# Attention and two mixture-of-experts layers on one core: a new step order for the attention, zero fills issued by SyncE, early constants spread over three pairs, one condition at the end

## The chip, the cores and the metric

The kernel runs on one core of a Trainium2 chip. The metric is the device time of one execution in microseconds (us). A core has a matrix engine (PE in the profile, TensorE), VectorE (DVE), ScalarE (ACT), GpSimd (POOL) and SyncE (SP), which issues most DMA transfers. Each engine works through its own queue of instructions in a fixed order, and semaphores make one engine wait for another.

## What is computed

```python
# q, k, v: (4, 12, 448, 64); x of the first layer is the attention's output, (1792, 768)
q_n, k_n = rmsnorm(q, g_q), rmsnorm(k, g_k)
attn = softmax(q_n @ k_n.T / 8);  x = attn @ v
# layer 1: 8 experts, D=768, F=1024, each token goes to its best expert
logits = x @ w_gate; e = argmax(logits); gate = softmax(logits)[e]
x = gate * sigmoid(x @ w_output_gate)[e] * (relu(x @ w1[e]) @ w2[e])
# layer 2: the same without the output gate, with a bias per modality
logits = x @ w_gate2 + modality_bias[modality_id]; e = argmax(logits)
out = softmax(logits)[e] * (relu(x @ w1b[e]) @ w2b[e])
```

## The kernel before

The attention works on 24 pairs of heads (two heads side by side on the 128 partitions), six pairs to each of the 4 batches. `Attn.do(name, i)` issues one step of pair i. A step's name tells its work, and each belongs to one engine:

- `ld`, `ldv` (SP, L540/541): loads of q, k and v for two pairs. `nsq` (ACT, L560), `nss` (DVE, L565), `ny0` to `ny2` (ACT, L568 to L570), `nt1`, `nt2` (DVE, L574, L577), `nmul` (POOL, L583): the root mean square and the scaling.
- `tpe` (PE, L591), `thi` (ACT, L594/595), `tlo` (DVE, L598/599): transposes into Z, split into a high and a low half. `stk` (SP, L606/607): four DMAs copy Z into the stacked operand T.
- `mpe0` to `mpe3` (PE, L614/616): scores for the maximum, all in one PSUM buffer psm. `mred0` to `mred3` (DVE, L619/L620): the maximum of each row into m. `rpe` (PE, L626/627): m becomes a row; `rcp` (ACT, L629) copies that row into T.
- `spe` (PE, L637/638): the scores into PSUM pst. `exp` (ACT, L642). `lo` (POOL, some on DVE, L645): the exponentials' low half plo. `vhi`, `vlo` (L553, L555): v split. `pv` (PE, L655 to L657): the av matmuls, 24 to a block. `ev`, `es` (L660 to L667): division by the sum.
- `xpe`, `xcp`, `lpe`, `ladd`: transposes of the result and the router's logits. `store` (SP, L497/498).

`Attn.order` sorts all steps by a key, which is `i + OFF[step]`, or for pairs at both ends an entry of the table `PRO`. A third table, `EXT`, gives keys to what is placed among them: the routing of the third batch (`rb`, `ra`, `rk`, `rs`), the pick of the first expert (`pk`, `ex`) and its loads and splits (`ld`, `lw`, `wh`, `wl` and others). Twelve ticks a pair run `tick`: it issues set-up loads and the routing of the first two batches (small DVE steps, L89 to L156, a few per tick). `hook` issues one zero fill of the buffer yd (L76, 384 KB from a tile of zeros, on ACT's queue) for each of pairs 6 to 19. The program is issued in the order of the keys, and that is each engine's order. Constants (L42 to L54 and L810 to L818, on POOL) are made ahead of pair 0's steps.

Then units of tokens of one expert follow: `halves` multiplies with w1 (eight blocks), yields (the middle), and with w2 (six blocks), all by `mm3` (L356). A unit's last scatter (L365, POOL) is put off to the next unit, or issued by `flush`. In the middle of unit e3 stands a condition (L965) for rare further units, whose body isn't run here. The end:

```python
seq=S["B"][:4]+S["S"]
for j in range(4): M.unit(seq[j],nx=seq[j+1],fx=seq[j+2],...)
M.flush()
NS=nc.values_load(nsi[0:1,0:1],min_val=0,max_val=E)      # L983
NB=nc.values_load(nbi[0:1,0:1],min_val=0,max_val=G2)     # L984
# chains: with tc.If(NS>i): M.unit(S[i], now=True); chains(i+1)    L985 to L992
# chainb: with tc.If(NB>i): a further unit; chainb(i+1), from i=4   L993 to L999
```

With this input NS is 2 and NB is 4: units B0 to B3 (304 tokens each) run in straight code, S0 and S1 (128 each) in nested conditions, and the conditions for more are not taken.

Of the kernel before, what the change touches and what calls it, by code (L numbers as in the profile page):

```python
# [27 lines left out]
class Moe:  # L28
# [471 lines left out]
class Attn:  # L500
# [182 lines left out]
    OFF=dict(ld=-3.47005,nsq=-2.879,nss=-2.54025,ny0=-2.4295,ny1=-2.42643,ny2=-2.3877,nt1=-2.36309,nt2=-2.36284,nmul0=-2.04952,  # L683
        nmul1=-2.04952,tpe0=-1.91912,thi0=-1.82412,tlo0=-1.80912,tpe1=-1.73278,thi1=-1.55,tlo1=-1.52437,mpe0=-1.23853,mred0=-1.11883,mpe1=-0.89826,
        mred1=-0.61069,mpe2=-0.58025,mred2=-0.49799,stk=-0.40471,mpe3=-0.39269,mred3=-0.36259,rpe=-0.28877,rcp=-0.05802,spe0=0.03615,exp0=0.22883,
        spe1=0.2646,spe2=0.31037,spe3=0.4246,exp1=0.44482,lo0=0.48909,ldv=0.50817,exp2=0.56868,exp3=0.57203,vhi=0.58407,vlo=0.75941,
        lo1=0.82029,lo3=0.95048,lo4=0.95048,lo6=0.95048,lo2=1.02771,lo5=1.06696,pv0=1.36506,pv1=1.42944,pv2=1.67538,pv3=1.83832,
        ev0=2.0046,ev1=2.07284,ev2=2.12131,es=2.3119,xpe=2.51876,xcp=2.67122,lpe=3.17606,ladd=3.42453,store=5.55173)
# [340 lines left out]
```

## Time and profile before

| | |
|---|---|
| median of 3 runs (lowest to highest) | 931.42 us (931.07 to 934.42) |
| the profiled execution, its own time | 930.19 us |
| its span, first to last instruction | 928.5 us |
| mean granted clock of TensorE, share of full speed | 0.967 |

The profile is of one execution. Its page groups busy time by engine and by line; the trace behind it has each instruction with its start, its length, and how long its engine stood idle before it and for whom. The page's line numbers are those of the kernel before; in the changed kernel the attention's lines stand 7 later.

### The profile page before, as it was taken

What the parts mean: (1) busy time and instruction counts of PE and PEld (TensorE: products, weight loads), DVE (VectorE), ACT (ScalarE), POOL (GpSimd) and SP (SyncE); (2) the same over time, 40 slices, a digit from 0 to 9 for tenths busy, and PEclk for the clock granted to TensorE, in tenths of its full rate; (3) what the DMA queues carried; (4) which work ended last, traced back from release to release, by engine and by line L of the source; (5) the groups of instructions that cost most, each with busy time, mean ns of one, the idle gap of its engine ahead of it and who ended that gap; (6) DMA issues with size and microseconds to landing.
All of it is one profiled execution on the core that took longest, in us unless ns stands there. A gap on an engine that the chain in (4) does not pass through costs nothing. (4 is left out here: it accounts for less than half of the span.)

```text
span 928.5 us, 23302 instructions
## 1 busy us (share of the span) xinstructions
PE 852.6 (92%) x8881; PEld 664.3 (72%) x8881; DVE 679.9 (73%) x1405; ACT 527.6 (57%) x967; POOL 386.9 (42%) x404
## 2 busy tenths in 40 slices
PE   4699998998998899999999999989989999999990
PEld 1366665665655788777788999887757777777890
DVE  6688889888778774877788888788646675655670
ACT  4577776776766542655455566565436454544560
POOL 5686767867766422413144242524023331411200
PEclk9799999999999899999999999999989999999996
DMA  5577655764564646995868779976748778594640
GB/s 129 122 169 171 166 169 146 187 167 118 135 169 133 168 133 201 268 282 211 218 177 326 234 164 317 310 208 233 240 131 259 232 284 185 223 310 136 243 157 13
DMA packets 143946, 182.00 MB, mean 196 GB/s; under 512 B 73736, under 2 KB 111384, under 8 KB 143808
## 3 DMA queue, kind: packets, MB, share of 16 engines
q1 hardware_dynamic: 131904, 151.95, 55.3%
q0 software_dynamic: 6784, 22.32, 8.0%
q10 hardware_dynamic: 5120, 5.98, 1.9%
q8 instruction: 76, 1.25, 0.6%
q14 instruction: 62, 0.51, 0.2%
HBM read 130.12 MB, written 24.33 MB: 166 GB/s over the span
## 5 line engine op out<-in xcount | busy, mean ns | idle before, releaser
L356 PE MATMUL pl<-XT,w1h 128*128 128x304 bf16 (+7 forms) x1632 | 259.3, 268 | 1.1 <-issue 0.5
L356 PE MATMUL pl<-hl,w2h 128*128 128x304 bf16 (+7 forms) x816 | 213.5, 270 | 6.3 <-DVEq L965 3.7
L356 PE MATMUL pl<-hh,w2h 128*128 128x304 f16 (+7 forms) x816 | 213.2, 269 | 0.0
L356 PE MATMUL pl<-hh,w2l 128*128 128x304 f16 (+7 forms) x816 | 213.2, 269 | 0.0
L356 PE MATMUL pl<-XT,w1l 128*128 128x304 f16 (+7 forms) x816 | 211.6, 268 | 1.2 <-issue 1.0
L356 PEld LDWEIGHTS <-w2h 128*128 128x128 f16 x1632 | 150.9, 98 | 35.7 <-issue 5.4
L356 PEld LDWEIGHTS <-w1h 128*128 128x128 f16 x1632 | 150.0, 98 | 29.1 <-issue 3.3
L645 POOL TENSOR_TENSOR plo<-p 128x448 f16<-128x448 f32 x142 | 140.1, 1005 | 52.1 <-ACT p L642 47.6
L299 DVE TENSOR_TENSOR w1l<-r,w1h 128x1024 bf16<-128x1024 f32 x96 | 116.6, 1229 | 45.6 <-ACT w1h L298 43.2
L423 ACT COPY yt<-pl 128x304 f32<-128x304 f32 (+7 forms) x102 | 37.0, 363 | 154.3 <-PE pl L356 147.6
L345 POOL TENSOR_TENSOR XS<-xr,XS 128x768 bf16<-128x768 f32 (+5 forms) x27 | 47.9, 1794 | 149.9 <-ACT XS L344 149.9
L298 ACT CAST w1h<-r 128x1024 f16<-128x1024 f32 x96 | 99.6, 1054 | 0.1
L642 ACT ACTIVATE p<-pst,eb 128x896 f32<-128x896 f32 (+1 forms) x96 | 86.4, 911 | 17.7 <-PE pst L638 16.8
L359 ACT ACTIVATE hh<-pl 128x304 f16<-128x304 f32 (+7 forms) x136 | 50.5, 372 | 75.5 <-PE pl L356 66.5
L655 PE MATMUL av<-vv,p 128*128 128x65 f16 (+1 forms) x768 | 89.4, 199 | 2.0 <-ACT xrow L667 2.0
L356 PEld LDWEIGHTS <-w2l 128*128 128x128 bf16 x816 | 80.2, 98 | 13.2
L356 PEld LDWEIGHTS <-w1l 128*128 128x128 bf16 x816 | 79.8, 98 | 13.1 <-DVE w1l L299 0.4
L655 PEld LDWEIGHTS <-p 128*128 128x128 bf16 (+1 forms) x768 | 73.4, 102 | 20.8 <-issue 14.8
L657 PE MATMUL av<-vv,plo 128*128 128x65 f16 (+1 forms) x768 | 87.6, 195 | 0.6 <-DVE plo L645 0.6
L656 PE MATMUL av<-vv,p 128*128 128x64 f16 (+1 forms) x768 | 88.1, 197 | 0.0
L619 DVE TENSOR_REDUCE m<-psm 128x2 f16<-128x896 f32 x70 | 76.0, 1086 | 10.0 <-PE psm L614 7.9
L299 DVE TENSOR_TENSOR w2l<-raw,w2h 128x768 bf16<-128x768 f32 x64 | 71.8, 1121 | 9.5 <-ACT w2h L298 9.3
(297 smaller groups left out, 1661.8 us busy)
## 6 DMA issues: line engine op xcount, KB each, us to landing
r<-in_moe_w_dram SPq DMA_DIRECT2D x96, 512.0 KB
raw<-in_moe_w_dram SPq DMA_DIRECT2D x64, 384.0 KB
r2a<-in_moe_w_dram SPq DMA_DIRECT2D x32, 384.0 KB
r2b<-in_moe_w_dram SPq DMA_DIRECT2D x32, 384.0 KB
T<-Z SPq DMA_DIRECT2D x48, 224.0 KB
T<-Z SPq DMA_DIRECT2D x48, 112.0 KB
yd<-zero ACTq DMA_DIRECT2D x14, 384.0 KB
rv<-in_v_dram SPq DMA_DIRECT2D x24, 192.0 KB
```

The lines of the kernel that those rows point to most:

```text
L298: if part!=1: nc.scalar.copy(h,t)
L299: if part!=0: (eng or nc.vector).tensor_tensor(out=l,in0=t,in1=h,op=ALU.subtract)
L345: if part!=0: (eng or nc.vector).tensor_tensor(out=self.XS[:m,t,1].bitcast(BF16),in0=x,in1=h,op=ALU.subtract)
L356: self.nc.tensor.matmul(p,a,b,start=i==0,stop=i==tot-1); i+=1
L359: nc.scalar.activation(h,p,AF.Relu)
L423: nc.scalar.copy(self.yt[:,db,:N],p)
L619: if t<3: nc.vector.tensor_reduce(m[:,t:t+4:3],p[:,:,:S],axis=AX.X,op=ALU.max,negate=True)
L642: self.nc.scalar.activation(self.d["P",i][:,self.u(kt)],p[:,:nn,:S],AF.Exp,bias=self.eb,scale=0.125)
L645: eng.tensor_tensor(out=self.d["L",i][:,u],in0=P[:,u],in1=self.hi(P)[:,u],op=ALU.subtract)
L655: nc.tensor.matmul(o,hh,w[:,0:65],start=kt==0,stop=False)
L656: nc.tensor.matmul(o[:,0:64],hh,w[:,65:129],start=False,stop=False)
L657: nc.tensor.matmul(o,ll,w[:,0:65],start=False,stop=kt==3)
```

## The change

The tables `OFF`, `PRO` and `EXT` have new numbers, so the attention's steps stand in another order (`PRO` now covers pairs 0 to 3 and 17 to 23, before 0 to 4 and 18 to 23). The limits of the routing's ticks move with them. `blank` issues its fill on SP's queue and is called from `tick` at the fifth tick of a pair. `consts`, `set_caps` and `early` become generators, and one piece of them is issued per tick of pairs 1 to 3. At the end S0 and S1 run in straight code behind B3; VectorE works out `over`, the number of units beyond these, in B1; every engine loads it in S0, and one condition on it stands in the middle of S1, with all further units in its body.

```diff
@@ class Moe @@
     def consts(self):
...
+        yield
         self.e8m=iota("e8m",[128,E],[[1,E]],-8,0)
+        yield
...
     def blank(self,t,i,n):
...
-        self.nc.scalar.dma_start(out=t[i*(NT//n):(i+1)*(NT//n),:]...
+        self.nc.sync.dma_start(out=t[i*(NT//n):(i+1)*(NT//n),:]...
...
     def redo(self,u,nx):
...
-        u.e=e; self.fetch(nx,nx.slot); nx.e=None; self.bring(nx,0,3)
-        nx.e=None
+        u.e=e
+        if nx is not None: self.fetch(nx,nx.slot); nx.e=None; self.bring(nx,0,3); nx.e=None
@@ class Attn @@
-    OFF=dict(ld=-3.47005,nsq=-2.879,nss=-2.54025,ny0=-2.4295,...
+    OFF=dict(ld=-3.56465,nsq=-2.18384,nss=-1.88231,ny0=-1.59399,...
...
@@ body_full @@
-            M.consts()
+            yield from M.consts()
...
+            yield from M.set_caps(CAPS,((128,0),(N2,128)))
...
         def rk(p,i):
-            if S.get("w")=="rk" and i<19: S["w"]=S["r"].send(p)
+            if S.get("w")=="rk" and i<16: S["w"]=S["r"].send(p)
         def rr(i):
-            if S.get("w")=="r" and i<19: step()
+            if S.get("w")=="r" and i<16: step()
         def tick(i,s):
             if i==0 and s in (1,3,5): M.clear_rows(s//2)
+            if 1<=i<4: next(S["e"],None)
+            if s==4 and 6<=i<20: M.blank(yd,i-6,14)
...
-            if "r" in S and i<19 and (S.get("w") is None or S["w"]=="sc" and s in (2,10)): step()
+            if "r" in S and i<21 and (S.get("w") is None or S["w"]=="sc" and s in (2,6,10)): step()
         def hook(i,s):
-            if s==2 and 6<=i<20: M.blank(yd,i-6,14)
+            pass
...
-            early(); A.run(O=O,EXT=EXT,ext=ext)
+            S["e"]=early(); A.run(O=O,EXT=EXT,ext=ext)
...
-        seq=S["B"][:4]+S["S"]
-        for j in range(4): M.unit(seq[j],nx=seq[j+1],fx=seq[j+2],...
+        seq=S["B"][:4]+S["S"][:2]
+        (be,nbi),(se,nsi)=S["b2"],S["s2"]
+        over=cst.tile([128,1],I32,name="over")
+        def more():
+            a,b=[lp.tile([128,1],F32,name=n) for n in ("ova","ovb")]
+            nc.vector.tensor_scalar(a,nsi,-2.0,0.0,op0=ALU.add,op1=ALU.max); nc.vector.tensor_scalar(b,nbi,-4.0,0.0,op0=ALU.add,op1=ALU.max)
+            nc.vector.tensor_tensor(out=over,in0=a,in1=b,op=ALU.add)
+        def load(t,n): return nc.values_load(t[0:1,0:1],min_val=0,max_val=n)
+        def chain(n,i,m,unit):
+            if i>=m: return
+            with tc.If(n>i):
+                u=unit(i); cold(u); M.unit(u); M.flush()
+                chain(n,i+1,m,unit)
+        def others():
+            post,M.post,sl=M.post,None,M.slot
+            with tc.If(S["over"]>0):
+                chain(load(nsi,E),2,E,lambda i: Unit(L2,se,i,128))
+                chain(load(nbi,G2),4,G2,lambda i: Unit(L2,be,i,N2))
+                M.redo(seq[-1],None)
+            M.slot=sl; M.post=post
+        def known(): S["over"]=load(over,E+G2)
+        sides={0:{KF+i:[stepper("table3")] for i in range(6)},1:{2:[more]},4:{2:[known]}}
+        for j,u in enumerate(seq):
+            M.unit(u,nx=seq[j+1] if j<5 else None,fx=seq[j+2] if j<4 else None,side=sides.get(j),late=0,mid=others if j==5 else None)
         M.flush()
-        (be,nbi),(se,nsi)=S["b2"],S["s2"]
-        NS=nc.values_load(nsi[0:1,0:1],min_val=0,max_val=E)
...
-        chains(0)
...
-        chainb(4)
```

The tables' effect is seen in the order of instructions. First SP's queue near the start: T_148 is the stacked operand of pair 1, wgt the gate weights, raw_114 the q and k of pairs 4 and 5. Before:

```order
L606 DMA T_148<-Z_154 64x2x896
L607 DMA T_148<-Z_154 64x2x448
L606 DMA T_148<-Z_154 64x2x896
L607 DMA T_148<-Z_154 64x2x448
L822 DMA wgt<-in_moe_w_gate_dram 128x6x8
L823 DMA wgt<-in_moe_w_output_gate_dram 128x6x8
L540 DMA raw_114<-in_q_dram 64x4x256
L541 DMA raw_114<-in_q_dram 64x4x192
L540 DMA raw_114<-in_k_dram 64x4x256
L541 DMA raw_114<-in_k_dram 64x4x192
```

and after the change:

```order
L837 DMA wgt<-in_moe_w_gate_dram 128x6x8
L838 DMA wgt<-in_moe_w_output_gate_dram 128x6x8
L613 DMA T_148<-Z_154 64x2x896
L614 DMA T_148<-Z_154 64x2x448
L613 DMA T_148<-Z_154 64x2x896
L614 DMA T_148<-Z_154 64x2x448
L547 DMA raw_114<-in_q_dram 64x4x256
L548 DMA raw_114<-in_q_dram 64x4x192
L547 DMA raw_114<-in_k_dram 64x4x256
L548 DMA raw_114<-in_k_dram 64x4x192
```

The two loads of gate weights moved from behind pair 1's stacking to ahead of it. Next TensorE's queue where pair 10's row of maxima (m_155) is made; Z_153 is pair 10's operand, Z_154 pair 11's, p and plo the exponentials of an earlier pair. Before, its last maximum block (L616), a block of 24 av matmuls and the row:

```order
L616 LDWEIGHTS Z_153
L616 MATMUL psm<-Z_153 64x448
...
L655 LDWEIGHTS p_1935
L655 MATMUL av<-vv_139,p_1935 128x65
...
L657 LDWEIGHTS plo
L657 MATMUL av<-vv_139,plo 128x65
L626 LDWEIGHTS m_155
L626 MATMUL pmt<-id_157,m_155 1x128
```

After the change the row stands behind the second maximum block of pair 11 (the blocks ahead of that, back to pair 10's last maximum block, are scores, av, pair 11's first maximum block, a transpose and two blocks of av):

```order
L664 LDWEIGHTS plo
L664 MATMUL av<-vv_139,plo 128x65
L621 LDWEIGHTS Z_154
L621 MATMUL psm<-Z_154 128x448
L633 LDWEIGHTS m_155
L633 MATMUL pmt<-id_157,m_155 1x128
```

Last VectorE's queue at pair 10's fourth maximum (the reduction that fills one column of m_155, L620), while a batch is routed (rt names); m_156 is pair 11's. Before:

```order
L619 TENSOR_REDUCE m_155<-psm 128x2
L131 TENSOR_REDUCE rt_o<-rt_a 128x4
L574 SCALAR_TENSOR_TENSOR y_2313<-ss,y_2313 128x16
L577 SCALAR_TENSOR_TENSOR rs<-y_2313,y 128x16
L620 TENSOR_REDUCE m_155<-psm 128x1
L134 TENSOR_TENSOR rt_r<-rt_r,rt_oh 128x32
L136 TENSOR_REDUCE rt_ix<-rt_r 128x4
L555 SCALAR_TENSOR_TENSOR vv_140<-rv_135,vv_140 128x8x64
L140 TENSOR_TENSOR rt_ixi<-rt_ix,iv 128x4
L619 TENSOR_REDUCE m_156<-psm 128x2
```

and after the change:

```order
L136 TENSOR_TENSOR rt_a<-rt_oh,lgs 128x32
L652 TENSOR_TENSOR plo<-p_1963 128x448
L138 TENSOR_REDUCE rt_o<-rt_a 128x4
L141 TENSOR_TENSOR rt_r<-rt_r,rt_oh 128x32
L627 TENSOR_REDUCE m_155<-psm 128x1
L143 TENSOR_REDUCE rt_ix<-rt_r 128x4
L606 SCALAR_TENSOR_TENSOR Z_154<-ptq,Z_154 128x448
L584 SCALAR_TENSOR_TENSOR rs<-y_2226,y 128x16
L147 TENSOR_TENSOR rt_ixi<-rt_ix,iv 128x4
L562 SCALAR_TENSOR_TENSOR vv_140<-rv_135,vv_140 128x8x64
L626 TENSOR_REDUCE m_156<-psm 128x2
L154 TENSOR_SCALAR rt_den<-rt_s 128x4
```

The two Newton steps (L574, L577) that stood right ahead of that maximum now stand apart from it, one behind it, and behind it come pair 11's low half and its first maxima.

## Rows read from the trace of the kernel before

**Rows 1.** The page, busy time of engines, and one group of section 5.

```profile
PE 852.6 (92%) x8881; PEld 664.3 (72%) x8881; DVE 679.9 (73%) x1405; ACT 527.6 (57%) x967; POOL 386.9 (42%) x404
...
L619 DVE TENSOR_REDUCE m<-psm 128x2 f16<-128x896 f32 x70 | 76.0, 1086 | 10.0 <-PE psm L614 7.9
```

**Rows 2.** Windows: stretch, length, busy time of each engine, clock, DMA share, GB/s.

```profile
core 0: us, PE busy (x) PEld busy (x) DVE busy (x) ACT busy (x) POOL busy (x), PEclk, DMA share, GB/s
18.37:48.39 30.02, 22.09 (x158) 10.00 (x157) 17.99 (x26) 16.79 (x31) 16.47 (x22) 0.77 0.41 95
104.52:126.72 22.20, 22.19 (x298) 15.26 (x297) 19.40 (x33) 17.46 (x33) 16.59 (x17) 1.00 0.62 162
126.72:166.06 39.34, 35.49 (x451) 23.82 (x450) 34.55 (x63) 26.55 (x49) 28.59 (x29) 0.96 0.61 170
199.28:239.96 40.68, 36.81 (x451) 24.28 (x450) 33.88 (x62) 26.92 (x49) 28.08 (x28) 0.92 0.54 144
262.68:302.20 39.52, 35.01 (x419) 21.81 (x417) 30.96 (x67) 23.78 (x42) 25.50 (x28) 0.91 0.53 142
302.20:323.06 20.86, 17.20 (x285) 14.53 (x283) 15.78 (x26) 12.40 (x18) 9.02 (x8) 0.84 0.60 149
690.59:695.90 5.31, 5.31 (x22) 3.18 (x22) 0.00 (x0) 0.00 (x0) 0.00 (x0) 0.50 0.62 191
909.15:928.50 19.35, 0.00 (x0) 0.00 (x0) 0.00 (x0) 0.00 (x0) 0.00 (x1) 0.55 0.05 14
```

**Rows 3.** Timelines of VectorE and TensorE, pair 11: start, length, instruction, idle before.

```profile
151.02 2.47 DVE L574 SCALAR_TENSOR_TENSOR y<-ss,y 128x16 f32<-128x16 f32 x1 [0.83 <-ACT vv L553]
154.36 0.19 PE L627 MATMUL pmt<-id,m 64*1 64x64 f16 x1 [1.84 <-DVE m L620]
```

**Rows 4.** Windows, a stretch of routing between pairs 9 and 10.

```profile
132.10:136.50 4.40, 4.40 (x39) 2.58 (x39) 3.66 (x9) 2.62 (x5) 2.03 (x3) 0.61 0.90 274
```

**Rows 5.** Timelines of TensorE and VectorE, a regular pair (pair 8).

```profile
107.54 0.37 PE L614 MATMUL psm<-Z 64*128 64x448 f16 x2
...
111.73 0.36 PE L614 MATMUL psm<-Z 64*128 64x448 f16 x2
...
114.09 0.38 PE L616 MATMUL psm<-Z 64*64 64x448 f16 x2
...
115.99 0.36 PE L614 MATMUL psm<-Z 64*128 64x448 f16 x2
...
110.08 1.21 DVE L565 TENSOR_REDUCE ss<-qn 128x16 f32<-128x1024 f32 x1
```

**Rows 6.** Timelines near the start: SP's queue, VectorE, ScalarE and POOL.

```profile
24.61 1.07 SPq L822 DMA_DIRECT2D wgt<-in_moe_w_gate_dram  x1
...
26.43 0.63 SPq L540 DMA_DIRECT2D raw<-in_q_dram  x1
...
21.36 0.62 DVE L599 SCALAR_TENSOR_TENSOR Z<-ptq,Z 128x448 f16<-128x448 f32 x1 [2.58 <-ACT Z L595]
...
33.09 1.06 ACT L560 ACTIVATE qn<-raw 128x1024 f32<-128x1024 f32 x1 [4.69 <-DMA raw<-in_k_dram]
34.05 1.51 ACT L642 ACTIVATE p<-pst,eb 128x448 f32<-128x448 f32 x2
...
13.60 2.04 POOL L583 TENSOR_TENSOR qn<-raw,rs 128x512 f32<-128x512 f32 x2 [0.33 <-DMA raw<-in_k_dram]
```

**Rows 7.** By line, the zero fills: nanoseconds least, median, most; first and last start.

```profile
L76 ACTq DMA_DIRECT2D yd<-zero x14: 520/521/527, 99.1 to 258.2; - x14
```

**Rows 8.** Timelines of TensorE in unit e3 and of POOL at the end.

```profile
690.59 0.41 PE L356 MATMUL pl<-hl,w2h 128*128 128x304 bf16 x1 [3.73 <-DVEq L965]
...
908.18 0.97 POOL L365 DMA_INDIRECT out_dram<-yr,idx  x1 [15.72 <-DVE yr L414]
```

**Rows 9.** By line, POOL's queue at the end (L987: condition of S0/S1; L1025: the kernel's end).

```profile
L987 POOLq INC_SWDGE_SEM  x1: 2470/2470/2470, 911.9 to 911.9; - x1
...
L1025 POOLq DRAIN  x3: 46/108/9460, 918.2 to 928.2; - x3
```

More of the change, by code (lines that the diff above doesn't have):

```diff
@@ L47, in consts @@
         nc.gpsimd.affine_select(self.tri,self.ones,pattern=[[1,128]],compare_op=ALU.is_gt,fill=0.0,base=0,channel_multiplier=-1)
+        yield
         self.e8m=iota("e8m",[128,E],[[1,E]],-8,0)
+        yield
         self.ecap=iota("ecap",[128,E],[[NT,E]],0,0)
+        yield
         self.pos3=iota("pos3",[128,3],[[128,3]],0,1)
+        yield
         self.e8=iota("e8",[128,E],[[1,E]],0,0)
+        yield
         self.d88=iota("d88",[128,E,E],[[1,E],[-1,E]],0,0)
+        yield
         self.g16=iota("g16",[128,16],[[1,16]],0,0)
+        yield
         self.zero=c.tile([128,384],F32,name="zero"); nc.gpsimd.memset(self.zero,0.0)
@@ L75, in blank @@
         a=NT//n//128 if n<=14 else None
-        self.nc.scalar.dma_start(out=t[i*(NT//n):(i+1)*(NT//n),:].rearrange("(p a) (c d) -> p (a c) d",p=128,d=384),in_=bc(self.zero[:,:384].unsqueeze(1),[128,2*a,384]))
+        self.nc.sync.dma_start(out=t[i*(NT//n):(i+1)*(NT//n),:].rearrange("(p a) (c d) -> p (a c) d",p=128,d=384),in_=bc(self.zero[:,:384].unsqueeze(1),[128,2*a,384]))
     def new_ord(self,name):
@@ L276, in set_caps @@
         nc=self.nc; self.thr={}
-        for n,b in thr: self.thr[n,b]=self.iota(f"thr{n}_{b}",[128,(NT+n-1)//n],[[n,(NT+n-1)//n]],b,0)
+        for n,b in thr: self.thr[n,b]=self.iota(f"thr{n}_{b}",[128,(NT+n-1)//n],[[n,(NT+n-1)//n]],b,0); yield
         self.caps=self.cst.tile([128,len(caps)],F32,name="caps")
@@ L682 @@
     LV=(1,); LW=(6,)
[L683 to L688, printed above, removed]
+    OFF=dict(ld=-3.56465,nsq=-2.18384,nss=-1.88231,ny0=-1.59399,ny1=-1.44328,ny2=-1.41999,nt1=-1.36699,nt2=-1.04793,nmul0=-1.03008,nmul1=-0.66968,tpe0=-0.60083,
+        thi0=-0.47331,tlo0=-0.39298,tpe1=-0.43342,thi1=-0.26534,tlo1=-0.06580,mpe0=-0.07761,mred0=0.05215,mpe1=0.09711,mred1=0.13654,mpe2=0.32282,
+        mred2=0.51928,stk=1.15575,mpe3=0.62346,mred3=0.85858,rpe=1.10176,rcp=1.35824,spe0=1.56603,exp0=2.34171,spe1=1.43927,spe2=1.67396,spe3=2.31041,
+        exp1=1.59000,lo0=2.95230,ldv=0.65460,exp2=1.98518,exp3=2.45481,vhi=1.79175,vlo=2.03156,lo1=2.72545,lo3=1.96476,lo4=2.10903,lo6=2.77559,lo2=1.99968,
+        lo5=2.58477,pv0=3.00963,pv1=2.95702,pv2=3.13277,pv3=2.80246,ev0=3.19695,ev1=3.47764,ev2=3.53702,es=3.57549,xpe=3.95377,xcp=4.11860,lpe=4.41602,
+        ladd=4.63086,store=4.56965)
     ENG={**dict.fromkeys("ld ldv stk store".split(),"S"),**dict.fromkeys("nsq ny0 ny1 ny2 thi0 thi1 rcp exp0 exp1 exp2 exp3 vhi es xcp".split(),"A"),
@@ L721, in order @@
         return sorted(l)
-    NV=1; PRO={"ld:18":14.55173,"nsq:18":15.05893,"nss:18":15.41089,"ny0:18":15.57035,"ny1:18":15.57119,"ny2:18":15.65266,"nt1:18":15.66791,"nt2:18":15.69841,"nmul0:18":15.95048,
[59 rows of a table removed]
+    NV=1; PRO={"nsq:0":-19.27451,"nss:0":-14.85970,"nsq:1":-14.34392,"ny0:0":-10.73866,"ny1:0":-10.55898,"ld:2":-10.12587,"nss:1":-9.57279,"ldv:0":-9.49539,"ny2:0":-9.21964,"ny0:1":-8.52114,
[61 rows of a table added]
     def ext(self,f,n): f(n)
@@ L812, in early @@
             nonlocal c1,c2,payc,val,m64,ta,tb
-            M.consts()
+            yield from M.consts()
             m64=cst.tile([128,4,4,2],I32,name="m64"); nc.gpsimd.memset(m64[64:128,:,3,:],0)
             payc=cst.tile([128,4,4,PW],F32,name="payc"); nc.gpsimd.memset(payc,0.0)
+            yield
             val=cst.tile([128,4],F32,name="val"); nc.gpsimd.memset(val,1.0); nc.gpsimd.memset(val[64:128,3:4],0.0)
-            ta=M.iota("ta",[128,4,4],[[448,4],[1,4]],0,4); tb=M.iota("tb",[128,4,4],[[448,4],[1,4]],64,3)
+            yield
+            ta=M.iota("ta",[128,4,4],[[448,4],[1,4]],0,4)
+            yield
+            tb=M.iota("tb",[128,4,4],[[448,4],[1,4]],64,3)
+            yield
             c1=M.new_counts("c1"); c2=M.new_counts("c2")
-            M.set_caps(CAPS,((128,0),(N2,128)))
+            yield
+            yield from M.set_caps(CAPS,((128,0),(N2,128)))
         def setup():
@@ L978, in body_full @@
         M.unit(e3,nx=B0,fx=S["B"][1],side={0:[lambda: M.fetch_pay(B0)],2:[lambda: M.fetch_rows(B0)]},mid=mid,cut=True,late=1,fp=8,fr=9)
-        seq=S["B"][:4]+S["S"]
-        for j in range(4): M.unit(seq[j],nx=seq[j+1],fx=seq[j+2],side={KF+i:[stepper("table3")] for i in range(6)} if j==0 else None,late=0)
-        M.flush()
-        (be,nbi),(se,nsi)=S["b2"],S["s2"]
-        NS=nc.values_load(nsi[0:1,0:1],min_val=0,max_val=E)
-        NB=nc.values_load(nbi[0:1,0:1],min_val=0,max_val=G2)
-        def chains(i):
-            if i>=E: return
-            with tc.If(NS>i):
-                u=S["S"][i]
-                if i>1: cold(u)
-                M.unit(u,nx=S["S"][1] if i==0 else None,now=True)
-                chains(i+1)
-        chains(0)
-        def chainb(i):
-            if i>=G2: return
-            with tc.If(NB>i):
-                u=Unit(L2,be,i,N2); cold(u); M.unit(u); M.flush()
-                chainb(i+1)
-        chainb(4)
+        seq=S["B"][:4]+S["S"][:2]
[22 more added lines that the diff above has]
+            M.unit(u,nx=seq[j+1] if j<5 else None,fx=seq[j+2] if j<4 else None,side=sides.get(j),late=0,mid=others if j==5 else None)
+        M.flush()
         pin(tc,mark)
```

2 lines of the change are left out of this document (1 added, 1 removed), and 130 rows, old and new, of tables (EXT, NV).

## Prediction

> **What bounds the kernel now.** I read the page's busy line first: TensorE is busy for 92% of the span, VectorE for 73% [rows 1]. Such a share is an average over three parts (attention, first MoE layer, second), and the change is almost all in the first, so I cut that part where ScalarE starts to copy the row of maxima (L629), once per pair of heads [rows 2]. Each window runs from one such start to another. From pair 7 to pair 9 the two pairs take 22.20 us with 22.19 us of TensorE work: there TensorE is the bound, at 11.1 us per pair, and no order makes it faster. Other windows are longer than 11.1 us a pair. From pair 0 (18.37) to pair 23 (302.20) go 283.83 us for 23 pairs; at 11.1 it would be 255.3, so 28.5 us are lost. They lie in five places: pairs 0 to 2 take 30.02 (7.8 over), 9 to 12 39.34 (6.0 over), 15 to 18 40.68 (7.4), 20 to 23 39.52 (6.2), and 1.1 remain elsewhere. Those three later places are the ones where a batch's tokens are routed to experts, which adds small VectorE steps.
>
> In the routed places TensorE isn't short of work, it waits for VectorE's maxima. The matmul of the row of maxima waited 1.84 us for the fourth maximum (L620), and the step ahead of that maximum on VectorE, a small Newton step (L574, 128x16), took 2.47 us [rows 3]; what stretched it the trace doesn't say. [...]
>
> **The new order in the middle of attention.** Before, on TensorE, the row of maxima of pair i (L626) stands one 0.9 us block of av matmuls behind the pair's last block of scores for the maximum. In the new order seven blocks stand between: scores, av, the next pair's first maximum block, a transpose, av twice, the next pair's second. That is about 5.0 us (the gaps 2.0 and 2.7 worked out below, and 0.3 for the last block), so VectorE may be 4 us later before TensorE waits. What can come back is bounded by VectorE itself, which in the routed windows is busy 34.55 of 39.34 and 33.88 of 40.68 [rows 2], so 4.8 and 6.8 at most; in the third VectorE has room (30.96) and the 6.2 over the regular pace bounds it; with the 1.1 from elsewhere that is 18.9 in all. VectorE's order is fixed, some steps still wait for ScalarE in it, and the routing's longest chain stays. I take half: **-9.5**, between 0 and -18.9.
>
> Regular pairs must not get worse. One PSUM buffer (psm) serves all four maximum blocks, so each block waits for the maximum before it. In pair 8 the blocks start at 107.54, 111.73, 114.09 and 115.99 [rows 5]: gaps of 4.2, 2.4, 1.9 and, to close the period, 2.7. The same blocks, each with the length that the starts within this period give it, make gaps of 2.7, 2.4, 4.1 and 2.0 in the new sequence. A maximum takes 1.09 (L619, page) [rows 1]; in the 2.4 gap VectorE has the sum of squares (1.21) [rows 5] ahead of it, 2.3 together. It fits by 0.1: cost 0, with a rival below.
>
> **Start, pairs 0 to 2.** The chain to pair 1's row of maxima (35.6, behind the exponentials that start at 34.05) goes over SP's loads of the gate weights (24.61 to 26.43, 1.8), which stand ahead of the load for pair 4; ScalarE's square for pair 4 waits 4.69 for that load's k, and two exponentials (1.51) stand behind it and ahead of the copy. Before all this VectorE waited 2.58 for ScalarE's high half of pair 1 [rows 6], which was queued behind pair 0's copy of maxima. The new order puts the weights ahead of pair 1's stacking, the high half ahead of that copy, and the exponentials behind pair 1's. It also puts pair 1's square ahead of pair 0's square root: +1.06 at worst, by the same kind of row (1.06) [rows 6]. Sum 1.8+2.6+1.5-1.1 = 4.8; something else will then be last, so **-4.5**, between +1 (only the square) and -7.8 (all of the loss).
>
> **Constants.** POOL made them up to 13.3 us; its next step, the scaling of pair 1, waited only 0.33 and for a DMA [rows 6], so it can't start earlier by more. In pairs 1 to 3, where they go, POOL is busy 16.47 of 30.02 [rows 2]. Their cover is that idle time; without it these some 40 small instructions, half of what POOL did until then, would hold up its low halves by up to 7 us. **0**, between -0.3 and +7.
>
> **Zero fills.** On ScalarE each issue took 520 ns, 14 in all [rows 7]: 7.3 us, hidden, since the queue issues while the engine still runs its last activation. On SP some nine DMA issues stand in each pair; at 520 ns they make 4.7 of 11.1 us, so one more fits. The new place is right behind a stack transfer (T) and ahead of a load. **0**, between -7.3 and the rival's price.
>
> [...]
>
> **Tail, pair 23 to the first expert.** 302.20 to 323.06 takes 20.86 with 17.20 of TensorE [rows 2], so 3.7 at most to gain. On SP six weight loads (five of 512 KB, one of 384: 2.94 MB) now stand ahead of pair 23's stacking, where two did. At the 274 GB/s of [rows 4] that is 10.7 us; TensorE's steps between that point and the scores that need it make about 10.5. **0**, between -4 and +4.
>
> **The end.** Before, units S0 and S1 each stand in a condition of their own, then comes a third. After the last scatter (908.18) POOL waits until 911.9, spends 2.47 on a semaphore of the condition, the same again at the third, and reaches its DRAIN at 918.2, which lasts 9.46 [rows 8, 9]. Without conditions behind the scatter the stretch 911.9 to 918.2 goes: -6.4. In its place a condition stands in the middle of S1. The same kind stands in the middle of unit e3: TensorE idle 3.73 [rows 8], then 5.31 us at clock 0.50 [rows 2], 2.65 of it lost: +6.4. Straight code at the two boundaries gives 0.4 each (a wait of 0.33 and a flush): -0.8, so **-1**. Bounds: -13 if the drain is bookkeeping of the conditions and shrinks, the middle costing nothing less; +1 if boundaries give nothing and the new small VectorE steps show.
>
> **Sum.** -9.5-4.5+0+0+0-1 = -15.0 against the profiled execution's 930.19: 915.2. The median of the runs is 931.42, 1.2 above it: 916.
>
> **Rivals.**
> 1. VectorE stays the bound in routed pairs: their pace is set by its chain through ScalarE, not by the distance on TensorE. For it: VectorE is busy 88% and 83% of two of them; against it: 30.96 of 39.52 in the third [rows 2]. The middle term is 0: 926, the edge of what can be told.
> 2. The single psm buffer makes regular pairs slower (the other side). Place: the 2.4 us gap, where 2.3 of VectorE work has 0.1 to spare. If the square is 1 us late from ScalarE, TensorE waits that in each of 17 regular pairs: +17, and the middle's gain goes as well: 916+17+9.5 = 942. It turns the sign from (4.5+1)/17 = 0.3 us a pair if the middle's gain is gone, from 0.9 if that is kept. For it: the thin margin. Against it: VectorE has 1.4 us idle per pair (19.40 of 22.20), which the same gap can use.
> 3. The last DRAIN shrinks with the conditions: 9.5 more, 907. For it: 9.46 us with nothing else running [rows 2, 9]. Against it: it stands at the kernel's very end, outside every condition.
> 4. Fills hold up T: 384 KB at 274 GB/s is 1.4 us, 14 times 20 us, so 936. That is only so if T is needed at once; in the new order the stacking of a pair can start a period, 11.1 us, before its scores; less 2.1 for four issues and 2.5 for 672 KB at 274 GB/s it has 6.5 us to spare, which covers 1.4. [...]
>
> **Chances.** My forecast 0.55; routed pairs stay bound by VectorE 0.17; drain shrinks 0.14; psm buffer 0.11; fills 0.03. Faster by over 0.5% (what a measurement here can tell; below 926.8): forecast, drain and a third of rival 1, less a little: 0.74. Within 0.5%: two thirds of rival 1 and half of rival 4: 0.14. Slower (above 936.1): 0.12. The likeliest case alone spans 905 to 925 (half of the middle's bounds and of the start's either way); with 1 and 3 the range is 902 to 932, and leaves out rival 2, rival 4 and a thin low end, under 2 in 10.
>
> **What would show it.** Right: copies of the row of maxima about 11.1 to 12 us apart in routed pairs; no TensorE wait for the fourth maximum at the row of maxima; the wait of ScalarE's square for pair 4 well below 4.69; no ScalarE issue of fills; a TensorE gap of about 3.7 us in the middle of S1 with clock 0.50 behind it; POOL's DRAIN some 6 us earlier after the last scatter. Wrong: TensorE waits for the maxima in regular pairs (rival 2); VectorE idle less than 1 us in a routed pair at the old pace (rival 1); waits for T before the scores (rival 4 and tail).

## The result, and the profile after the change

The changed kernel takes 945.16 us (median of 4 runs, 942.87 to 947.39) against 931.25 us before (930.13 to 934.42). The ratio is 1.0144, 95% interval 1.0108 to 1.0179: slower, where 916 was forecast and 902 to 932 was the range. Its profiled execution took 945.89 us with a span of 943.80, 15.3 longer than before.

First the page's busy line of the changed kernel, the answer to [rows 1].

```profile
PE 855.6 (91%) x8881; PEld 668.5 (71%) x8881; DVE 661.6 (70%) x1408; ACT 528.9 (56%) x967; POOL 380.3 (40%) x404
```

It says almost nothing: TensorE does 3 us more in a span of 15 more, so about 12 are waits, somewhere. Windows tell where. I cut the changed kernel's trace at the same places as in [rows 2], at the copies of the row of maxima (now L636). The columns are those of [rows 2]; x after a busy time is the number of instructions, for PE the matmuls.

```profile
22.04:41.04 19.00, 16.79 (x98) 7.18 (x96) 16.06 (x23) 14.34 (x24) 13.74 (x47) 0.91 0.77 173
114.69:127.01 12.32, 11.29 (x150) 7.73 (x149) 9.35 (x22) 8.87 (x17) 7.62 (x9) 1.00 0.37 97
41.04:265.06 224.02, 204.26 (x2682) 138.46 (x2679) 168.08 (x315) 158.60 (x290) 152.50 (x155) 0.99 0.61 153
265.06:340.30 75.24, 56.05 (x746) 38.42 (x745) 46.26 (x93) 38.61 (x65) 37.93 (x37) 0.84 0.51 135
```

For the last two, from pair 2 to pair 20 and from there to the first expert's first matmul, the kernel before has these windows:

```profile
48.39:262.68 214.29, 205.09 (x2671) 137.88 (x2669) 186.01 (x316) 159.76 (x294) 156.12 (x152) 0.98 0.63 162
262.68:323.06 60.38, 52.20 (x701) 36.34 (x699) 46.74 (x92) 36.18 (x59) 34.52 (x35) 0.89 0.55 144
```

Now the 15.3 can be laid out by the starts of such copies and of POOL's scatters. Pair 2's copy comes 7.35 earlier than before (41.04 for 48.39): the start won. From pair 2 to pair 20 it loses 9.73 (224.02 for 214.29), from pair 20 to the first expert 14.86 (75.24 for 60.38). From there to the last scatter but one 3.46 more (571.40 for 567.94), in S1's middle 3.66 (20.84 for 17.18), and behind the last scatter it wins 9.06 (11.26 for 20.32). The sum: -7.35+9.73+14.86+3.46+3.66-9.06 = +15.30.

These copies don't stand at equal work, since the new order moves work across them: up to pair 2's copy the changed kernel has done 128 matmuls and the one before 182, up to pair 20's copy 2804 and 2851. At pair 5's copy (76.74 after, 80.78 before) the counts are 619 and 618, at pair 16's (214.49 and 213.19) both are 2256. Windows from pair 5 to pair 16 and from there to the first expert, two after and two before:

```profile
76.74:214.49 137.75, 125.71 (x1639) 85.53 (x1638) 100.31 (x203) 97.99 (x181) 90.40 (x92) 0.99 0.62 158
214.49:340.30 125.81, 100.17 (x1294) 67.57 (x1293) 85.07 (x154) 73.19 (x127) 72.45 (x73) 0.91 0.54 139
80.78:213.19 132.41, 126.01 (x1640) 85.53 (x1639) 116.05 (x204) 97.14 (x181) 96.86 (x95) 0.97 0.63 168
213.19:323.06 109.87, 98.92 (x1295) 67.23 (x1293) 88.98 (x158) 72.56 (x124) 71.81 (x70) 0.92 0.55 142
```

At equal work the start has thus won 4.04, pairs 5 to 16 lose 5.34 and the stretch from pair 16 to the first expert loses 15.94; the sum stays +15.30. These are the numbers to hold against the forecast.

**The start.** ScalarE's square for pair 4 waits 0.34 for its load's k, where it waited 4.69:

```profile
30.75 1.06 ACT L567 ACTIVATE qn<-raw 128x1024 f32<-128x1024 f32 x1 [0.34 <-DMA raw<-in_k_dram]
```

**The middle.** TensorE's busy time from pair 2 to pair 20 is no larger than before (204.26 for 205.09); its idle time is 19.8 us where it was 9.2. The views of waits of TensorE in these windows name who was waited for: total, times, longest. The longest of the kernel after, then of the kernel before:

```profile
PE ptq L598 <- DVE lgs L687: 9.8, 11, 1.6
```

```profile
PE pmt L627 <- DVE m L620: 3.2, 2, 1.8
PE psm L614 <- DVE m L619: 3.0, 4, 1.1
```

The wait for the fourth maximum at the row of maxima (3.2) is gone, as forecast. But the transposes (L598) now wait for VectorE's step L687, eleven times, 9.8 us together. One regular pair shows why, in the timeline of TensorE and VectorE after:

```profile
116.31 0.36 PE L621 MATMUL psm<-Z 64*128 64x448 f16 x2
117.29 1.07 PE L683 MATMUL psm<-wgt,xt 128*128 128x16 f32 x8
120.68 0.72 PE L598 MATMUL ptq<-ident,qn 128*128 128x128 f32 x4 [0.81 <-DVE lgs L687]
...
118.39 1.09 DVE L626 TENSOR_REDUCE m<-psm 128x2 f16<-128x896 f32 x1 [2.07 <-PE psm L683]
119.40 0.55 DVE L671 TENSOR_TENSOR xrow<-av,rc 128x384 f32<-128x384 f32 x1
119.86 0.67 DVE L605 SCALAR_TENSOR_TENSOR Z<-ptq,gg,Z 128x448 f16<-128x448 f32 x1
120.45 0.21 DVE L687 TENSOR_TENSOR lgs<-lgs,psm 128x64 f32<-128x64 f32 x1
```

The third maximum block is written at 116.31 and done at 116.7. Its maximum (L626) starts only at 118.39: VectorE stood idle 2.07 us, and by the profile for L683. That is `lpe`, the router's logits, eight small matmuls that write into the same PSUM tile psm and now stand between the block and its maximum on TensorE. All of VectorE's queue behind it comes later by that: a division, the low half (L605) that empties ptq, the addition of the logits. So the next transposes wait 0.81. The regular pair takes 12.32 us (window 114.69:127.01) where it took 11.1.

**The tail.** In 265.06 to 340.30 TensorE's idle time is 19.2 us, before it was 8.2; that makes 11.0 of the 14.9. The rest is busy time: the clock is lower (0.84 for 0.89), and 45 more matmuls lie in the window. The views of waits after, of TensorE and of SP's queue:

```profile
PE pst L644 <- DMA T<-Z: 8.4, 2, 5.6
PE pst L644 <- ACT p L649: 4.0, 3, 2.0
PE av L664 <- POOL plo L652: 3.7, 2, 3.2
...
SPq L333 <- DMA o<-payc,rt_ixi: 15.0, 1, 15.0
```

And the rows around it, SP's queue and TensorE:

```profile
307.25 0.34 SPq L333 DMA_DIRECT2D pay<-o  x1
...
308.68 1.89 SPq L309 DMA_DIRECT2D r<-in_moe_w_dram  x2
310.69 0.64 SPq L613 DMA_DIRECT2D T<-Z  x1
...
319.21 0.53 PE L644 MATMUL pst<-T 128*128 128x448 f16 x1 [5.59 <-DMA T<-Z]
```

SP waits 15.0 us at L333, the fetch of the first expert's payload (`fp0`), until the routing's scatter has written it. Two weight loads and then the stacking of pair 23 (L613, 310.69) are queued behind, and the scores of pair 23 wait 5.59 for T.

**The end**, in timelines of TensorE and POOL and in the lines' view of POOL's queue:

```profile
921.09 0.27 PE L363 MATMUL pl<-hl,w2h 128*128 128x128 bf16 x1 [3.49 <-DVEq L1012]
...
932.54 0.97 POOL L372 DMA_INDIRECT out_dram<-yr,idx  x1 [19.21 <-DVE yr L421]
...
L1048 POOLq DRAIN  x3: 46/109/10672, 932.3 to 943.6; - x3
```

The condition in S1's middle shows as a gap of 3.49, close to the 3.73 of [rows 8]; over the next 5.31 us the clock is 0.71, where 0.50 was forecast. The DRAIN begins right at the last scatter (932.3), and lasts 10.67 us: it did not shrink.

### The profile page after: what moved, and what is told of

Same layout as the page of the kernel before. It is cut to its first block, busy times and chain, and to the rows that moved or that the text cites. A ratio compares the mean times of both kernels' runs of the same rounds, so it can differ in the third digit from the quotient of the medians.

```text
span 943.8 us, 23252 instructions
## 1 busy us (share of the span) xinstructions
PE 855.6 (91%) x8881; PEld 668.5 (71%) x8881; DVE 661.6 (70%) x1408; ACT 528.9 (56%) x967; POOL 380.3 (40%) x404
## 5 line engine op out<-in xcount | busy, mean ns | idle before, releaser
L363 PE MATMUL pl<-XT,w1h 128*128 128x304 bf16 (+7 forms) x1632 | 262.5, 270 | 2.8 <-DMA XT<-XS 1.4
L652 POOL TENSOR_TENSOR plo<-p 128x448 f16<-128x448 f32 x142 | 135.1, 971 | 73.7 <-ACT p L649 68.4
L626 DVE TENSOR_REDUCE m<-psm 128x2 f16<-128x896 f32 x70 | 76.3, 1090 | 44.3 <-PE psm L683 25.5
```

Of the source, the lines that this page charges most:

```text
L363: self.nc.tensor.matmul(p,a,b,start=i==0,stop=i==tot-1); i+=1
L626: if t<3: nc.vector.tensor_reduce(m[:,t:t+4:3],p[:,:,:S],axis=AX.X,op=ALU.max,negate=True)
L652: eng.tensor_tensor(out=self.d["L",i][:,u],in0=P[:,u],in1=self.hi(P)[:,u],op=ALU.subtract)
```

## The experiments

A ratio is always to the kernel before on the same chip, with its 95% interval. Single executions of one kernel spread by some 0.5% either way here. My theories after the result were two: `lpe` ahead of the maximum costs the middle, and the new order of pairs 17 to 23 costs the tail. Their rivals: VectorE's own load or the fills for the middle, and for the tail the one wait for T behind `fp0`.

**1. lpe away from the maximum.** The changed kernel, with `lpe` moved behind the third maximum in the regular pairs:

```diff
-  OFF: ... xcp=4.11860,lpe=4.41602,
+  OFF: ... xcp=4.11860,lpe=4.52500,
+  PRO: "lpe:0":4.525, "lpe:2":6.525, "lpe:3":7.525; lpe of pairs 13 to 16, 22, 23 as before this edit
```

> The changed kernel, with the router's matmul (lpe) of pairs 0 and 2 to 12 put behind the third maximum (mred2) of the pair whose PSUM buffer it writes to, where it stood ahead of that maximum and behind its scores. Theory A (the maximum waits for the router's matmul in its buffer, 2.07 us in a regular pair, and the transposes of the next pair wait for VectorE behind it, 0.81): the period of regular pairs falls from 12.32 to 11.1 to 11.3 us, about 10 to 12 periods, so 945 goes to 931 to 934. Theory B (VectorE's fixed order with its waits for ScalarE is too tight in any case, as my prediction's rival put it at another gap): the period stays above 12 and the time at 943 to 946.

929.38 us, ratio 1.0031 (1.0005 to 1.0057), for the change's 1.0144. Windows of this run: pairs 7 to 9, the three routed pairs from 9 to 12 one by one, pairs 5 to 16, from there to the first expert, and from pair 20 to the first expert. Then TensorE's waits in 119.38 to 158.00, in which these two are all:

```profile
97.47:119.38 21.91, 21.91 (x298) 15.47 (x297) 18.03 (x37) 17.95 (x33) 15.57 (x17) 1.00 0.75 195
119.38:130.46 11.08, 11.08 (x155) 7.86 (x154) 10.45 (x28) 8.98 (x17) 8.02 (x9) 1.00 0.83 215
130.46:142.02 11.56, 11.02 (x150) 7.82 (x149) 10.11 (x17) 8.97 (x16) 8.88 (x10) 1.00 0.36 98
142.02:158.00 15.98, 13.73 (x150) 9.81 (x149) 12.79 (x17) 8.97 (x16) 13.22 (x14) 0.79 0.73 198
75.53:202.56 127.03, 123.79 (x1639) 87.40 (x1638) 105.79 (x203) 98.71 (x181) 89.95 (x92) 0.97 0.66 172
202.56:324.65 122.09, 99.11 (x1294) 66.59 (x1293) 84.12 (x154) 73.11 (x127) 72.45 (x73) 0.93 0.54 143
253.94:324.65 70.71, 53.89 (x746) 37.16 (x745) 45.77 (x93) 38.56 (x65) 37.92 (x37) 0.90 0.51 143
```

```profile
PE av L664 <- DVE plo L652: 2.3, 1, 2.3
PE psm L621 <- DVE m L626: 0.5, 1, 0.5
```

A regular pair is back at 10.95 us with TensorE never idle, and pairs 5 to 16 take 127.03 where the change took 137.75: 10.7 less, 1.0 per pair. So `lpe` was the cause of the middle's loss, and with it mended 5.4 of the forecast's gain show (132.41 before). The edit leaves `lpe` of pairs 13 to 16 where the change had it, so between pairs 16 and 20 five maxima still wait for L683, 0.5 to 2.1 us each. From pair 16 to the first expert it takes 122.09, 12.2 more than before (from pair 20 on 70.71 for 60.38), which eats the gain: a second cause.

The routed pairs gained and lost. Pairs 9 to 10 and 10 to 11 took 13.97 and 13.89 before, now 11.08 and 11.56; but pair 11 to 12 takes 15.98 for 11.48. In it TensorE waits 2.3 for VectorE's low half plo, and its clock is 0.54 in the last 5.2 us. Ahead of that low half stands a small Newton step on VectorE (L581). The rows of VectorE and POOL there, then POOL's of the kernel before beside the step of [rows 3]:

```profile
146.54 4.00 DVE L581 SCALAR_TENSOR_TENSOR y<-ss,y 128x16 f32<-128x16 f32 x1
146.89 3.60 POOL L652 TENSOR_TENSOR plo<-p 128x448 f16<-128x448 f32 x4
```

```profile
150.72 2.73 POOL L645 TENSOR_TENSOR plo<-p 128x448 f16<-128x448 f32 x3
```

The step takes 4.00 us and ends 0.05 behind POOL's run of four low halves (150.54 and 150.49). The step of 2.47 us in [rows 3], which the prediction found unexplained, ends as close behind POOL's run of three (153.49 and 153.45). That POOL's run is what stretches it is likely from these rows, but no run moved one away from the other.

**2. lpe ahead of the maximum, in the kernel before.** The same fault alone, put into the old order for pairs 5 to 12:

```diff
-  OFF: ... lpe=3.17606,ladd=3.42453
+  OFF: ... lpe=3.46000,ladd=3.52000
+  PRO: lpe of 13 to 17, 22, 23 and ladd of 13 to 16 at their old keys
```

> The kernel before, with the router's matmul of pairs 5 to 12 moved between a third block of scores for the maximum and its maximum, with two blocks between, as the changed kernel has it in its own order. Theory A (the maximum waits for the router's matmul on the same buffer): VectorE's third maximum in those periods waits some 2 us for that matmul, the fourth block 0.5 to 1 us, regular periods go from 11.0 to 11.5 to 12 us, 4 to 8 us slower in all. Theory B (in the changed kernel it was another neighbour that cost the time): periods stay at 11.0 to 11.1.

946.3 us, ratio 1.0165 (1.0126 to 1.0204). A regular pair here (first window), the stretch behind its wait (second), and the rows of VectorE and TensorE:

```profile
171.36:185.30 13.94, 12.63 (x150) 8.38 (x149) 10.14 (x17) 8.62 (x16) 10.24 (x11) 0.87 0.51 131
184.50:187.50 3.00, 3.00 (x38) 1.86 (x35) 3.00 (x3) 2.10 (x3) 3.00 (x4) 0.55 0.79 184
```

```profile
181.87 1.09 DVE L619 TENSOR_REDUCE m<-psm 128x2 f16<-128x896 f32 x1 [2.45 <-PE psm L676]
183.14 0.38 PE L616 MATMUL psm<-Z 64*64 64x448 f16 x2 [0.83 <-DVE lgs L680]
```

The same wait appears (2.45 for L676, the old number of `lpe`'s line), and by pair 15 the kernel is 14.7 us late. The price is 2.9 us a pair, not 1.2: 1.3 are waits, and 1.6 more is busy time, because the granted clock falls to 0.55 behind the wait (1.00 from 177.50 to 183.10, 0.74 from there to 184.50, 1.00 again from 187.50).

**3. Pair 23's stacking earlier.** The wait for T in the tail suggests one edit: give `stk:23` its place ahead of what holds SP. Four places were tried, ahead of all weight loads in the changed kernel, and ahead of the payload's fetch or behind two loads, with `lpe` mended or not:

```diff
-  "stk:23":26.37501
+  "stk:23":25.20000   (the change; ahead of six weight loads)
+  "stk:23":25.30000   (experiment 1's kernel; behind two loads)
+  "stk:23":25.86500   (experiment 1's kernel, and the change; behind four loads, ahead of fp0)
```

> The changed kernel, with pair 23's four stacking DMAs (stk) put ahead of the six weight loads on SP. Theory A (TensorE's waits of 5.59 and 2.82 us for T before pair 23's scores come from the loads queued ahead): both waits go, the first unit starts 7 to 8 us earlier, 945 goes to 937 to 938. Theory B (the loads that now start later are last instead, and the first unit waits for its weights): within 2 us of 945.

> The kernel with the router's matmul behind the maximum, and pair 23's stacking on SP behind the first two weight loads and ahead of the other four. Theory A (the waits of 4.32 and 2.21 us for T come from the four loads ahead, and the earlier attempt failed since the first load's split stands on ScalarE ahead of pair 22's copy): both waits go, 4 to 6 us faster, 924. Theory B (whatever stands ahead, SP waits at the stacking for Z and the loads behind it come late, so that ScalarE waits for them): no gain, 928 to 932.

> The kernel with the router's matmul behind the maximum, and pair 23's stacking on SP just ahead of the fetch of the first unit's payload (fp0), behind the first four weight loads. In the changed kernel's trace SP waits 15.0 us at that fetch for the routing's scatters to land, and the stacking stands behind it. Theory A (that wait on SP, not the loads, makes T late): the waits of 4.32 and 2.21 us go, no load comes later, and the first unit starts 5 to 7 us earlier: 922 to 925. Theory B (another chain of the tail is as long: routing, scatters, gathers of the first unit): the waits for T go, others of the same length come, no change.

> The changed kernel as it is, with pair 23's stacking ahead of the payload fetch. Theory A: its waits of 5.59 and 2.82 us for T go, 945 becomes 937 to 939. Theory B: no change.

In this order: 1.0184 (1.0142 to 1.0226), 1.0024 (0.9996 to 1.0051), 1.0026 (0.9998 to 1.0053) and 1.0141 (1.0083 to 1.0200): none better than its parent (1.0144 or 1.0031). The wait for T was gone in each, and others stood in its place. Of the first, ScalarE's timeline; of the last, TensorE's view of waits in the tail:

```profile
303.45 1.04 ACT L305 CAST w1h<-r 128x1024 f16<-128x1024 f32 x1 [7.50 <-DMA r<-in_moe_w_dram]
```

```profile
PE av L664 <- POOL plo L652: 6.7, 3, 3.0
PE pst L644 <- ACT p L649: 6.6, 4, 2.6
```

Weights that come later hold ScalarE's casts, which stand ahead of a copy of maxima in its queue; POOL's low halves and the exponentials come late as well. The wait for T is one of several chains of about the same length, not the cause by itself.

**4. The old order of the tail.** The keys of pairs 18 to 23 and of `EXT` from the kernel before, in experiment 1's kernel. The first try moved only `EXT` (keys of before + 1.59; the pairs' keys stayed those of the change), so its edit is less than its expectation says:

> The kernel with the router's matmul behind the maximum (first experiment of this study), and for pairs 18 to 23 and what is placed among them (routing of the last batch, pick, first unit's loads and splits) the order of the kernel before, its keys moved by 1.39 and 1.59. Theory A (the other loss lies in the new order of the tail alone): from pair 20's copy of the maxima to the first unit's first matmul it takes 60 to 63 us as before (60.4), where it took 70.7, so the gain of 8 us at pair 20 stays and the time is 8 to 10 us below that kernel, 918 to 921. Theory B (the tail is slower because the new middle ends in another state, whatever the order behind it): the stretch stays above 67 and the time within 3 us of that kernel.

930.93 us, 0.9993 (0.9959 to 1.0026): nothing gained. It reached pair 20 at 249.62, but the first expert's matmul only at 324.72. ScalarE waited again for weights:

```profile
269.72 1.04 ACT L305 CAST w1h<-r 128x1024 f16<-128x1024 f32 x1 [7.78 <-DMA r<-in_moe_w_dram]
```

Then both tables, with the keys of before moved by 1.35:

```diff
-  PRO: pairs 17 to 23 of the change;  EXT of the change
+  PRO: pairs 18 to 23 of the kernel before (and its four keys of pair 17), + 1.35;  EXT of the kernel before, + 1.35
```

> The kernel with the router's matmul behind the maximum, and now truly the order of the kernel before for pairs 18 to 23 and for the last batch's routing, the pick and the first unit's loads and splits, all keys moved by 1.35 (the earlier attempt, f1, moved only the loads, splits and routing among them; the pairs' own keys stayed the changed kernel's). Theory A (what is lost between pair 20 and the first unit lies in the new order of these two tables): the stretch from pair 20's copy of the maxima to the first unit takes 60 to 63 us as before, not 70.7; the gain of 8 to 10 us at pair 20 stays, and the time is 7 to 11 us below before, 0.988 to 0.993. Theory B (the new order in the middle, or what else the change does, makes the tail long whatever its order): above 67 us, and 0.998 to 1.004.

Here the stackings of pairs 18 and 19 overwrote T ahead of the last scores of pairs 16 and 17, which therefore were made from the wrong operand; the third try puts them behind and leaves nothing out:

```diff
-  stk:18, stk:19 by the moved keys
+  "stk:18":18.32, "stk:19":19.32
```

> As f2_tail (new order up to pair 17 with the router's matmul behind the maximum, the old order from pair 18 on), with the stacking of pairs 18 and 19 put behind the last scores of pairs 16 and 17, which read the same T (in f2_tail it stood ahead of them, so that these scores were made from the next pairs' T). Theory A: the same as f2_tail, 0.988 to 0.994 of before; from pair 20 to the first unit 59 to 62 us. Theory B: SP's later stacking gives back 2 us or more per pair, 0.995 to 1.

919.41 us, 0.9907 (0.9878 to 0.9935), and 919.49 us, **0.9880** (0.9845 to 0.9915): faster than both kernels. The tail's window in the one and in the other:

```profile
258.36:317.74 59.38, 50.65 (x700) 36.02 (x699) 46.35 (x92) 36.25 (x59) 35.01 (x35) 0.91 0.51 138
```

```profile
259.66:323.61 63.95, 55.11 (x700) 38.86 (x699) 46.45 (x92) 36.23 (x59) 34.45 (x35) 0.84 0.51 136
```

59.38 is the 60.38 of before, at equal work (2850 matmuls up to pair 20's copy, 2851 before); 63.95 stands in an execution of 928.61, the longest of seven with a median of 919.49, and has the same idle time (8.8 for 8.7) with a lower clock. But pairs 16 to 20 now take 56.40 in the first of the two, where the kernel before takes 49.49 (109.87 less 60.38):

```profile
201.96:258.36 56.40, 47.73 (x596) 32.51 (x595) 38.82 (x63) 37.24 (x66) 34.57 (x36) 0.97 0.49 119
```

From pair 16 to the first expert that is 115.78 together, 6.3 less than experiment 1's 122.09 and still 5.9 more than before. So the new numbers for pairs 17 to 23 and the steps placed among them, taken together, cost 6.3 of the 12.2 by these profiles (experiment 1's is of its shortest execution), and 10 us by the medians (929.38 and 919.49). What is left stays open: the seam between the two orders lies in pairs 16 to 20, and no run tested it. Nor were the old keys of the pairs timed with the changed `EXT`.

**5. The new end, alone.** The kernel before with the new end of the diff, run twice, and a third kernel without the count of further units and the condition on it (it leaves that unused part out):

```diff
-  the old end (values_load of NS and NB, chains(0), chainb(4))
+  the new end of the change's diff, redo too                      (run twice)
...
-  sides={...,1:{2:[more]},4:{2:[known]}}, mid=others
+  sides={...}, mid=None                                            (the third)
```

> The kernel before, with the end of the changed kernel alone (S0 and S1 straight, one condition in the middle of S1). From the traces of both: behind the last scatter 20.3 falls to 11.3 us, and S1 grows by 4.7, so theory A: 4 to 5 us faster than before, 926 to 927. Theory B (the sum of my prediction, -1): 930. In either case POOL's last drain stays 9 to 11 us long.

> The kernel before with the changed kernel's end once more, since its first interval reached from 5 us faster to no change. Theory A: 3 to 5 us faster than before, the interval below 1. Theory B: 1 us or less.

> The kernel before with the changed kernel's end, and without its one condition: the units beyond S1 are left out altogether, as is the number of them. Theory A (the condition in the middle of S1 costs what the trace shows there, 4 to 5 us, and nothing of the last drain): 4 to 5 us faster than the kernel before with that end, 6 to 9 faster than the kernel before, drain 9 to 11 us. Theory B (the drain is bookkeeping of conditions): the drain falls by several us as well, 12 or more faster than before.

0.9976 (0.9948 to 1.0004), 0.9980 (0.9953 to 1.0008) and 0.9898 (0.9855 to 0.9940). By the profiles the new end gains 3.1 of span in the first and 3.2 in the second; timed it is about 2 us, and each interval reaches 1. In the first, S1's second half starts behind the condition, in the timelines of TensorE and POOL:

```profile
901.32 0.26 PE L356 MATMUL pl<-hl,w2h 128*128 128x128 bf16 x1 [3.52 <-DVEq L995]
...
914.12 0.97 POOL L365 DMA_INDIRECT out_dram<-yr,idx  x1 [20.58 <-DVE yr L414]
```

From the last scatter but one to the last it takes 22.2 us, 16.3 in the kernel without the condition, and 17.2 before. In these two profiles the condition and its count thus cost 5.9; in the other kernels with the new end the same stretch takes 19.5 to 22.4, so 3 to 6 us is what the runs tell. Behind the last scatter both take 11.3, so the drain isn't the conditions' bookkeeping.

**6. Fills back on ScalarE's queue** (the changed kernel, otherwise whole), and **constants at once** (experiment 1's kernel):

```diff
-        self.nc.sync.dma_start(out=t[...
+        self.nc.scalar.dma_start(out=t[...
...
-            S["e"]=early(); A.run(O=O,EXT=EXT,ext=ext)
+            S["e"]=iter(tuple(early())); A.run(O=O,EXT=EXT,ext=ext)
```

> The changed kernel, with the 14 zero fills issued by ScalarE's queue again, at the place in the order that they have in it. Theory A (who issues the fills is hidden): 944 to 946. [...] Theory C (issues on ScalarE delay its exponentials): 4 to 7 us slower.

> The kernel with the router's matmul behind the maximum, with all of POOL's early constants made at once ahead of pair 0 as in the kernel before. Theory A (spreading them is worth nothing): within 1.5 us of that kernel, copies of the maxima of pairs 0 to 4 within 1 us of its. Theory B (spreading them is what makes pairs 1 and 2 earlier): pair 2's copy 3 us or more later, 3 to 7 us slower.

942.4 us, 1.0145 (1.0111 to 1.0180), against 1.0144 with the fills on SP; and 931.03 us, 1.0014 (0.9987 to 1.0042), against experiment 1's 1.0031 (1.0005 to 1.0057), with all copies of pairs 0 to 10 within 0.2 us of it. Neither edit is worth anything.

## Why the prediction was wrong, point by point

The sum's middle ran from pair 2 to pair 23, its tail from there to the first expert. By those copies the two are +17.1 (9.73 and 46.92-39.52) for -9.5, and +7.5 (28.32-20.86) for 0. But at these copies the two kernels have not done the same work, so I go by pairs 5 and 16, where they have.

**Middle: -9.5 forecast; +5.3 measured in pairs 5 to 16.** The step that failed is "Regular pairs must not get worse". It listed what each gap between maximum blocks holds on VectorE and took psm as used by those blocks alone. `lpe` writes into the same tile, and its place in the new order, between a block and that block's maximum, was not looked at. Rival 2 named the right buffer and the right sign, but the wrong gap: not the 2.4 us one behind a late square, but the 4.1 us one that looked safest. It forecast 17 times 1 us; a regular pair lost 1.2. That its 942 comes near the measured 945 is partly luck, since it held no loss in the tail.

The gain that was claimed is there in part. With `lpe` mended (experiment 1) pairs 5 to 16 take 5.4 less than before, and the wait at the row of maxima is gone, as forecast. But the gain isn't where the sum put it: 1.6 lie in pair 5 to 6, 2.2 in pair 15 to 16, and only 0.7 in the routed pairs 9 to 12 (38.62 for 39.34), where half of 4.8 was claimed. Two of these three pairs gave back 5.2, and the third lost 4.5 again, behind the Newton step of 4.00 us. Rival 1 gave 0 for the middle, since VectorE's chain through ScalarE sets the pace of routed pairs. Its time isn't borne out up to pair 16, nor is its reason: in pair 9 to 10 TensorE is busy 11.08 of 11.08. How much of the gain is left behind pair 16 the runs don't tell, since the tail's loss lies over it.

**Tail: 0 (-4 to +4) forecast from pair 23; +7.5 measured there, +15.9 from pair 16 on.** The sum counted the weight loads ahead of pair 23's stacking and their bandwidth. It did not count `fp0`, a DMA whose issue waits 15.0 us on SP for a scatter, with the stacking queued behind it. What the forecast said would show it, a wait for T, is there (8.4). But experiment 3 takes that wait away and gains nothing, so the term is wrong by more than that one row: the order from pair 17 on puts several chains (T, weights on ScalarE, POOL's low halves) late together, and the sum looked at one of them, and only from pair 23 on. Of the 15.9, 3.7 went with `lpe` (experiment 1: 12.2), and 6 by the profiles, 10 by the medians, with the old numbers (experiment 4). Which of the numbers cost it, and what the rest is, stays open.

**Start, -4.5 forecast, -4.0 measured at pair 5** (-5.25 with `lpe` mended: 75.53 for 80.78). The mechanism was right: ScalarE's square for pair 4 waits 0.34 for its load, where it waited 4.69 [rows 6]. The -7.35 at pair 2's copy is in part the cut: 98 matmuls lie between the copies of pairs 0 and 2 where 158 did [rows 2].

**End, -1 forecast, -5.4 by this profile, about -2 timed alone.** The condition in the middle was right within what the runs tell (6.4 forecast; 3 to 6 by experiment 5). The gain behind the scatter was too small: 9.1 where 6.4 and 0.8 were forecast, since the DRAIN now begins right at the last scatter: the 3.7 us that POOL waited up to 911.9 [rows 8, 9] went too, and only 1.2 came back in a longer DRAIN. Rival 3 fell: 10.67 us.

**Constants and fills, 0 forecast**: right, by experiment 6; rival 4 fell with it. Fills on SP or on ScalarE's queue make no difference that these runs can tell: 1.0144 and 1.0145.

Of the distance of 30.3 from -15 to +15.3, the attention behind pair 5 makes 30.8 (+21.3 for -9.5) and the start 0.5; the end gives back 4.4. The remaining 3.5 lie between the first expert and the last scatter but one, where the order is the same. Runs with the old attention or the old end show 0.8 to 4.0 there too, so I don't put it down to the change.

## What to carry to other kernels

When an order of work is changed, list for each shared PSUM tile everything that writes to it, small matmuls too, and see that nothing stands between a write and its reader: here 1 us of router matmuls cost 1.0 to 1.2 us in each pair. For each queue, list what waits in it, not only what it moves: here one DMA that waited 15.0 us for a scatter held two weight loads and pair 23's stacking behind it. Where several chains are about equally long, removing the wait that a profile shows last only uncovers the next (experiment 3), so go back to the whole order of that stretch. And compare two orders only where they have done equal work: the same two traces gave -7.35 for the start at one copy and -4.04 at another, and the count of matmuls up to the cut told which to trust.

## What the runs showed of the hardware that was not expected

Two waits of almost the same length had different prices. In the changed kernel TensorE waited 0.81 us in a pair and its granted clock stayed at 1.00 over that pair; in experiment 2 it waited 0.83 and, 1.4 us later, ran for 3.0 us at 0.55. What tells the two apart isn't settled.

The same Newton step on 128x16 values (L581) took 0.17 us at 120.88 in the changed kernel and 4.00 us in experiment 1, where POOL ran four low halves beside it. Two more stretched steps end within 0.05 us of such a run: L584, 2.08 us to 139.58 in experiment 1 (POOL's run to 139.55), and 3.21 us to 239.21 in the changed kernel (239.17).

The last DRAIN on POOL takes 9.46 us with conditions behind the scatter [rows 9] and 10.67 without: in both kernels it stands at the end, and what it waits for the trace doesn't say.
